# Augmented q and k on all 128 partitions, in a kernel of attention, a mixing MLP and gated expert attention

## The chip, the cores and the metric

The kernel runs on one core of one Trainium2 chip. The metric is the device time of one execution in microseconds (us); less is better. The five engines of the core run side by side, each through its own instructions in a fixed order, and wait for each other by semaphores: TensorE (PE: matrix products, which go to PSUM), VectorE (DVE), ScalarE (ACT), GpSimd (POOL) and SyncE (SP, which here issues most DMAs).

## The reference, cut to what matters

Three blocks follow each other. The first is causal attention with a forget gate, over 4 batches of 8 heads with 576 positions and head width 64:

```python
scores = scale * np.matmul(q, k.transpose(0, 1, 3, 2))
cum = np.cumsum(np.log(np.clip(f, 0.0001, 1.0)), axis=-1)
decay = cum[:, :, :, None] - cum[:, :, None, :]
scores = np.where(causal, -1000000000.0, scores + decay)
scores = scores - np.max(scores, axis=-1, keepdims=True)
attn = np.exp(scores)
attn = attn / (np.sum(attn, axis=-1, keepdims=True) + 1e-09)
return np.matmul(attn, v).astype(np.float32)
```

The second takes x (4 x 576 x 512), mixes positions by U and V (rank 32) and applies an MLP of width 2048: `u + np.maximum(u @ w_ch1, 0.0) @ w_ch2`. The third has four experts, each a causal attention with head width 64 and no decay, of which a gate picks two per position: `out += mask[..., None] * w[:, :, kk:kk + 1] * ye`.

## The kernel before, in words

Every float32 value that is multiplied is split into a high part that TensorE's format holds and a low rest, so most products come in threes (high by high, high by low, low by high).

A head has four tiles (make_heads, L115): qa and ka hold the high parts of q and k in partitions 0 to 63, qb and kb hold the low and high parts for the two cross products, on all 128 partitions. qa and ka are augmented: partitions 64 and 65 of ka hold the negated cumulative log gates (high and low), against ones in qa, which adds the column part of the decay inside the score product; partition 66 of qa holds the row's maximum, against -1 in ka, which subtracts it. AUG is 67: score products of qa and ka contract 67 partitions, those of qb and kb 128. The partitions behind AUG aren't read. In the expert block partitions 64 and 65 of ka are zero.

For each head row_max (L151) first forms all scores of the causal triangle on 66 partitions (ua, ub) and VectorE takes their maxima with a mask (L159, L177) into a column tile mx; TensorE transposes it (mt, L182), VectorE makes the row mr of it (L184), and two DMAs put mr into partition 66 of qa (L186, L187). Then scores (L190) forms the transposed scores again in two PSUM tiles: for u = 0 five products, for u = 1 twelve (L213), of qa by ka, qb by kb and the mask. ScalarE takes the exponential (pf, L222) and its half-precision part (ph, L223), VectorE the rest (pl, L224). weighted_values (L230) multiplies by the values (av, 45 products per head), and normalise (L287) writes x. Per head, 1600 columns of scores and 1600 columns of row maxima are products of qa and ka, 1600 of qb and kb, 576 of the mask, and some 2900 of av.

log_sums (L476) is the first thing in the program: it loads f, clips it (L484), takes the logarithm on ScalarE (L485), scans it on VectorE (L486), splits the result into chl (L487, L488), stores it (L490) and feeds partitions 64 and 65 of the first ka tiles by DMA (L549). Meanwhile load_pair (L518) loads q, k (qkt) and v (vr) of two heads by one pair of DMAs, split_high (L528) casts them on ScalarE, split_low (L540) copies rows by DMA and forms the low parts on GpSimd, and value_scale (L248) finds a power of two for v: a reduce (L251), a transpose by TensorE (amt), three small steps and a reciprocal, and the scaling of vr (L270).

first_batch (L701) works through the 8 heads of the first batch; mix (L582) turns each pair's x into u (gp, up), and behind it the weights of the MLP are loaded, and narrowed from the 64-bit words of their layout by steps on VectorE and ScalarE (L308 to L311; wst). later_batches (L735) puts the products of the MLP (hps, L399: hidden; cps, L414: output, evacuated by L416) between the heads of the other three batches. Behind the heads, at some 400 us, the rest of the MLP runs alone; then the expert block, from some 695 us, with six heads' tiles (heads2, two heads, made at some 400 us; heads3, four heads, made when the MLP's pools are released).

TensorE's order is written out by hand (manual_schedule). The order on VectorE, ScalarE, GpSimd and SyncE's queue is set by the framework's scheduler, which runs its own timeline model over the program; so an added instruction can change the order of others.

Of the kernel before, what the change touches and what calls it, by code (L numbers as in the profile page):

```python
# [18 lines left out]
P = 128  # L19
B, H, S, D = 4, 8, 576, 64  # L20
# [7 lines left out]
HC = 288  # L28
# [1 line left out]
KT = DM // P  # L30
NQ = 4
FT = FF // P // NQ
AUG = 67
NH2A = 2
NH2B = 4
PSCALE_LN = 8.0 * math.log(2.0)
# [14 lines left out]
M_LO = [0, 64, 192, 320, 448]  # L51
# [3 lines left out]
def f32(ap):  # L55
    return ap.bitcast(F32)
# [3 lines left out]
def kernel(  # L60
# [13 lines left out]
    nc = tc.nc  # L74
# [4 lines left out]
    def pool(name, bufs=1, side="left", space=None):  # L79
        kw = {} if space is None else {"space": space}  # L80
        if space is None:
            kw["side"] = side
            kw["reuse_waits"] = "tile"
        return tc.alloc_tile_pool(name=name, bufs=bufs, **kw)
# [27 lines left out]
    ones1 = const.tile([1, P], BF16, name="ones1")  # L112
    nc.gpsimd.memset(ones1[:], 1.0)

    def make_heads(pl_, n, decay):  # L115


        made = []
        for i in range(n):
            qa = pl_.tile([P, S], F32R, name=f"qa{i}")  # L120
            qb = pl_.tile([P, S], F32R, name=f"qb{i}")
            ka = pl_.tile([P, SP_], F32R, name=f"ka{i}")
            kb = pl_.tile([P, SP_], F32R, name=f"kb{i}")
            nc.gpsimd.memset(f32(qa[64:AUG, :]), 1.0)
            nc.gpsimd.memset(f32(ka[:, S:SP_]), 0.0)
            nc.gpsimd.memset(f32(kb[:, S:SP_]), 0.0)
            nc.gpsimd.memset(f32(ka[64:AUG, :S]), -1.0)
            if not decay:
                nc.gpsimd.memset(f32(ka[64:66, :S]), 0.0)
            made.append((qa, qb, ka, kb))  # L130
        return made

# [18 lines left out]
    def row_max(hb, mx, apart=False):  # L151


        qa, qb, ka, kb = hb
        ua = ps2.tile([P, 2, 512], F32, name="ua", tag="s2")
        for c0, c1 in ((0, HC), (HC, S)):
            nc.tensor.matmul(ua[:, c0 // HC, 0:HC], qa[0:66, M_LO[4]:S], ka[0:66, c0:c1],
                             start=True, stop=True)
        nc.vector.tensor_tensor_reduce(  # L159
            ua[:, :, 0:HC], ua[:, :, 0:HC],  # L160
            maskm[:].rearrange("p (c n) -> p c n", c=2), 1.0, NEG, OP.add, OP.max, mx[:, 4:5])
        if apart:
            yield
        ub = ps2.tile([P, 2, 512], F32, name="ub", tag="s2")
        where = {3: (0, 0), 0: (0, 448), 2: (1, 0), 1: (1, 320)}
        for t in (3, 2, 1, 0):
            bk, off = where[t]
            w = M_W[t]
            n = 64 if t == 0 else P
            nc.tensor.matmul(ub[0:n, bk, off:off + w], qa[0:66, M_LO[t]:M_LO[t] + n],  # L170
                             ka[0:66, 0:w], start=True, stop=True)
        for t in (3, 2, 1, 0):
            bk, off = where[t]
            w = M_W[t]
            n = 64 if t == 0 else P
            m0 = S - P if t == 0 else S - w
            nc.vector.tensor_tensor_reduce(  # L177
                ub[0:n, bk, off:off + w], ub[0:n, bk, off:off + w], maskm[0:n, m0:m0 + w], 1.0, NEG,
                OP.add, OP.max, mx[0:n, t:t + 1])
        yield  # L180
        mt = psf.tile([NT, P], F32, name="mt", tag="f")
        nc.tensor.transpose(mt[:], mx[:], ident[:])  # L182
        mr = small.tile([NT, P], F32R, name="mr", bufs=2)
        nc.vector.tensor_scalar(mr[:], mt[:], PSCALE_LN / ISC, None, OP.subtract)  # L184
        row = f32(qa[66:67, :])
        nc.sync.dma_start(row[:, 0:64], f32(mr[0:1, 0:64]))  # L186
        cur["last"] = nc.sync.dma_start(row[:, 64:S].rearrange("o (t p) -> o t p", p=P),  # L187
                                        f32(mr[1:NT, :]))

    def scores(hb):  # L190

        qa, qb, ka, kb = hb
        ph = cur["att"].tile([P, 1600], F16, name="ph")
        pl = cur["att"].tile([P, 1600], F16, name="pl")
        for u in range(2):
# [6 lines left out]

            todo = []
            for some in (pieces[:-1], pieces[-1:]):
                todo += [(ka[0:AUG, jt * P:jt * P + P], qa[0:AUG, i0:i0 + w], bk, off, w)
                         for jt, i0, bk, w, off in some]
                todo += [(kb[:, jt * P:jt * P + P], qb[:, i0:i0 + w], bk, off, w)
                         for jt, i0, bk, w, off in some]
# [3 lines left out]
            for n, (wa, xa, bk, off, w) in enumerate(todo):  # L212
                nc.tensor.matmul(ps[:, bk, off:off + w], wa, xa, start=bk not in banks[:n],  # L213
                                 stop=bk not in banks[n + 1:])
            if u == 0:
                todo = ((ps[:, :, 0:HC], 0, S),)
            else:
                todo = ((ps[:, 0, :], S, 512), (ps[:, 1, :], S + 512, 512))
# [278 lines left out]
    sin = pool("sin", 1)  # L497
    att = pool("att", 2)
    hpool = pool("heads1")
    heads = make_heads(hpool, 4, True)  # L500
    att0 = pool("att0", 1, "right")
    pf0 = pool("pf0", 3, "right")
    cur["pf"] = pf0
# [313 lines left out]
    hpool = pool("heads2")  # L817
# [24 lines left out]
                            fill=0.0, base=0, channel_multiplier=0)  # L842
    every = sw.tile([P, P], BF16, name="every")
    nc.gpsimd.memset(every[:], 1.0)
    heads = make_heads(hpool, NH2A, False)
    def load_y(b, yp, stp, tag):
        yh = yp.tile([P, KT, SP_], F32R, name="yh", tag="yh")
        yl = yp.tile([P, KT, SP_], F32R, name="yl")
# [15 lines left out]
    hpool2 = pool("heads3", 1, "right")  # L864
    att = pool("att2", 2, "right")
    cur["att"] = cur["pf"] = att
    sy = pool("sy", 2, "right")
    ys = [sy0, pool("sy1", 1, "right")]
    heads += make_heads(hpool2, NH2B, False)

    def gates(lg, cf):

# [339 lines left out]
```

## Time and profile before

| What | us |
|---|---|
| timed runs: lowest, median, highest of 3 | 910.83, 911.1, 919.22 |
| profiled execution, its own time | 907.14 |
| its span, first to last instruction | 905.4 |
| TensorE busy in the span | 836.5 |
| VectorE busy | 543.4 |
| ScalarE busy | 429.0 |
| GpSimd busy | 304.8 |

The profile is of one execution; its own time is the span and what lies around it. All times of instructions are counted from the start of the span. Busy time is the time in which an engine has an instruction under way; products of TensorE overlap, so the time of one product as listed is longer than what it adds. The granted clock is the share of full speed that TensorE was given: 1.00 is 2.4 GHz, 0.50 is 1.2 GHz.

### The profile page before, as it was taken

What the parts mean: (1) busy time and instruction counts of PE and PEld (TensorE: products, weight loads), DVE (VectorE), ACT (ScalarE), POOL (GpSimd) and SP (SyncE); (2) the same over time, 40 slices, a digit from 0 to 9 for tenths busy, and PEclk for the clock granted to TensorE, in tenths of its full rate; (3) what the DMA queues carried; (4) which work ended last, traced back from release to release, by engine and by line L of the source; (5) the groups of instructions that cost most, each with busy time, mean ns of one, the idle gap of its engine ahead of it and who ended that gap; (6) DMA issues with size and microseconds to landing.
All of it is one profiled execution on the core that took longest, in us unless ns stands there. A gap on an engine that the chain in (4) does not pass through costs nothing.

```text
span 905.4 us, 19022 instructions
## 1 busy us (share of the span) xinstructions
PE 836.5 (92%) x7476; PEld 785.1 (87%) x7476; DVE 543.4 (60%) x1464; ACT 429.0 (47%) x836; POOL 304.8 (34%) x283
## 2 busy tenths in 40 slices
PE   2888599989999999989999999999999999999997
PEld 2777498879999989989989999999999888989775
DVE  6789879986667756632254722222223768787654
ACT  3667566655544554332255622322112576665553
POOL 9556654443322442012145422523103241311000
PEclk9987779999999999999999999999999999999999
DMA  6335565453432442003169742433103231321222
GB/s 190 113 98 139 160 214 172 150 176 92 115 100 84 133 121 63 27 18 115 53 228 340 237 163 91 129 109 126 54 27 92 54 86 41 88 45 30 73 89 71
DMA packets 68809, 101.94 MB, mean 113 GB/s; under 512 B 6640, under 2 KB 49456, under 8 KB 68720
## 3 DMA queue, kind: packets, MB, share of 16 engines
q1 hardware_dynamic: 64448, 92.47, 34.1%
q10 hardware_dynamic: 4272, 8.26, 2.5%
q8 instruction: 59, 0.97, 0.4%
q14 instruction: 30, 0.25, 0.1%
HBM read 60.33 MB, written 22.56 MB: 92 GB/s over the span
## 4 chain that ended last, share of the span: by engine, by line
PE 69%; DVE 13%; DMA 8%; ACT 5%; issue 3%; SPq 1%; POOL 1%; ACTq 0%; DVEq 0%; POOLq 0%
PE cps L414 20%; PE hps L399 18%; PE sc L213 9%; PE pq L917 4%; PE po L1029 3%; DMA raw<-in_w_dram 3%; DVE pl L224 3%; PE av L240 2%; PE pv L982 2%; PE gp L588 2%; PE ub L170 2%; DVE ub L177 2%; ACT pf L222 2%; PE av L244 2%; PE av L242 2%
## 5 line engine op out<-in xcount | busy, mean ns | idle before, releaser
L414 PE MATMUL cps<-hh,w2h 128*128 128x288 f32 x512 | 155.7, 304 | 3.6 <-DVE hl L404 3.4
L224 DVE TENSOR_TENSOR pl<-pf,ph 128x576 f16<-128x576 f32 x144 | 124.8, 869 | 47.3 <-ACT ph L223 47.2
L414 PE MATMUL cps<-hh,w2l 128*128 128x288 f32 x512 | 152.3, 297 | 0.0
L414 PE MATMUL cps<-hl,w2h 128*128 128x288 f32 x512 | 151.6, 296 | 0.0
L399 PE MATMUL hps<-uh,w1h 128*128 128x288 f32 x512 | 144.2, 303 | 0.0
L404 DVE SCALAR_TENSOR_TENSOR hl<-hps,hh 128x288 fp32r<-128x288 f32 x128 | 58.2, 455 | 142.0 <-ACT hh L403 142.0
L399 PE MATMUL hps<-uh,w1l 128*128 128x288 f32 x512 | 141.1, 298 | 0.0
L403 ACT ACTIVATE hh<-hps 128x288 fp32r<-128x288 f32 x128 | 52.4, 409 | 182.9 <-PE hps L399 182.9
L222 ACT ACTIVATE pf<-sc 128x576 f32<-128x576 f32 x144 | 83.8, 612 | 41.6 <-PE sc L213 34.9
L414 PEld LDWEIGHTS cps<-hh,w2h 128*128 128x128 f32 x512 | 97.3, 190 | 4.7 <-DVE hl L404 4.5
L399 PEld LDWEIGHTS hps<-uh,w1h 128*128 128x128 f32 x512 | 97.3, 190 | 0.2 <-DVE hl L404 0.2
L399 PEld LDWEIGHTS hps<-uh,w1l 128*128 128x128 f32 x512 | 97.4, 190 | 0.0
L414 PEld LDWEIGHTS cps<-hh,w2l 128*128 128x128 f32 x512 | 97.1, 190 | 0.0
L414 PEld LDWEIGHTS cps<-hl,w2h 128*128 128x128 f32 x512 | 97.0, 189 | 0.0
L213 PE MATMUL sc<-qa,ka 67*128 67x288 f32 (+4 forms) x288 | 77.8, 330 | 15.0 <-DMA qa<-mr 7.7
L223 ACT CAST ph<-pf 128x576 f16<-128x576 f32 x144 | 89.1, 638 | 1.5
L240 PE MATMUL av<-vh,ph 128*128 128x65 f16 x720 | 88.1, 204 | 1.5 <-DVE x L287 1.5
L399 PE MATMUL hps<-ul,w1h 128*128 128x288 f32 x512 | 87.9, 294 | 0.0
L242 PE MATMUL av<-vl,ph 128*128 128x64 f16 x720 | 86.8, 199 | 0.0
L244 PE MATMUL av<-vh,pl 128*128 128x65 f16 x720 | 86.6, 199 | 0.0
L177 DVE CUSTOM_DVE_ANT_0 ub<-ub,maskm 128x448 f32<-128x448 f32 x192 | 81.4, 424 | 8.2 <-PE ub L170 7.0
L385 POOL TENSOR_TENSOR ul<-ust,uh 128x1152 fp32r<-128x1152 f32 x18 | 48.2, 2676 | 89.4 <-ACT uh L384 84.8
(182 smaller groups left out, 1986.7 us busy)
## 6 DMA issues: line engine op xcount, KB each, us to landing
raw<-in_w_dram SPq DMA_DIRECT2D x32, 512.0 KB
ust<-udram SPq DMA_DIRECT2D x20, 576.0 KB
qkt<-in_qk_dram SPq DMA_DIRECT2D x16, 576.0 KB
yc<-ydram SPq DMA_DIRECT2D x14, 576.0 KB
ydram<-yc SPq DMA_DIRECT2D x14, 576.0 KB
vr<-in_v_dram SPq DMA_DIRECT2D x16, 320.0 KB
udram<-ustage ACTq DMA_DIRECT2D x16, 288.0 KB
ydram<-ust SPq DMA_DIRECT2D x8, 576.0 KB
```

The lines of the kernel that those rows point to most:

```text
L177: nc.vector.tensor_tensor_reduce(ub[0:n, bk, off:off + w], ub[0:n, bk, off:off + w], maskm[0:n, m0:m0 + w], 1.0, NEG, OP.add, OP.max, mx[0 ...
L213: nc.tensor.matmul(ps[:, bk, off:off + w], wa, xa, start=bk not in banks[:n], stop=bk not in banks[n + 1:])
L222: nc.scalar.activation(pfv, view, AF.Exp, scale=ISC)
L223: nc.scalar.copy(ph[:, o0:o0 + n], pf[:, 0:n])
L224: nc.vector.tensor_tensor(pl[:, o0:o0 + n], pf[:, 0:n], ph[:, o0:o0 + n], OP.subtract)
L240: nc.tensor.matmul(av[0:m, it, :], ph[0:k, c:c + m], vh[0:k, jt, :], start=first, stop=False)
L242: nc.tensor.matmul(av[0:m, it, 0:64], ph[0:k, c:c + m], vl[0:k, jt, :], start=False, stop=False)
L244: nc.tensor.matmul(av[0:m, it, :], pl[0:k, c:c + m], vh[0:k, jt, :], start=False, stop=last)
L399: nc.tensor.matmul(ph[:], wa[:, k, fs], xa[:, k, :], start=n == 0, stop=n == 3 * KT - 1)
L403: nc.scalar.activation(hh[:], ph[:], AF.Relu)
L404: nc.vector.scalar_tensor_tensor(hl[:], ph[:], 0.0, f32(hh[:]), OP.max, OP.subtract)
L414: nc.tensor.matmul(pc[:], wa[:, t, dsl], xa[:], start=n == 0, stop=n == 3 * FT - 1)
```

## The change

qa and ka are filled on all 128 partitions, and AUG becomes 127: the row's maximum goes to partition 127 of qa (against -1 in ka), the decay stays in partitions 64 and 65. Partitions 66 to 95 have ones in qa and zeros in ka, partitions 96 to 126 zeros in qa and -1 in ka, so all of them add zero. The row-max products contract 127 partitions in place of 66, the score products of qa and ka 128 in place of 67. Each head's two tiles get two memsets on GpSimd (32 x 576 each, in place of 3 x 576; the separate zeroing of partitions 64 and 65 in the expert block is gone) and two on VectorE (32 x 576 each).

```diff
-AUG = 67
+AUG = 127
...
-    def make_heads(pl_, n, decay):
+    def make_heads(pl_, n):
...
-            nc.gpsimd.memset(f32(qa[64:AUG, :]), 1.0)
+            nc.gpsimd.memset(f32(qa[64:96, :]), 1.0)
+            nc.vector.memset(f32(qa[96:P, :]), 0.0)
             nc.gpsimd.memset(f32(ka[:, S:SP_]), 0.0)
             nc.gpsimd.memset(f32(kb[:, S:SP_]), 0.0)
-            nc.gpsimd.memset(f32(ka[64:AUG, :S]), -1.0)
-            if not decay:
-                nc.gpsimd.memset(f32(ka[64:66, :S]), 0.0)
+            nc.gpsimd.memset(f32(ka[64:96, :S]), 0.0)
+            nc.vector.memset(f32(ka[96:P, :S]), -1.0)
             made.append((qa, qb, ka, kb))
         return made
...
-            nc.tensor.matmul(ua[:, c0 // HC, 0:HC], qa[0:66, M_LO[4]:S], ka[0:66, c0:c1],
+            nc.tensor.matmul(ua[:, c0 // HC, 0:HC], qa[0:AUG, M_LO[4]:S], ka[0:AUG, c0:c1],
                              start=True, stop=True)
...
-            nc.tensor.matmul(ub[0:n, bk, off:off + w], qa[0:66, M_LO[t]:M_LO[t] + n],
-                             ka[0:66, 0:w], start=True, stop=True)
+            nc.tensor.matmul(ub[0:n, bk, off:off + w], qa[0:AUG, M_LO[t]:M_LO[t] + n],
+                             ka[0:AUG, 0:w], start=True, stop=True)
...
-        row = f32(qa[66:67, :])
+        row = f32(qa[AUG:P, :])
...
-                todo += [(ka[0:AUG, jt * P:jt * P + P], qa[0:AUG, i0:i0 + w], bk, off, w)
+                todo += [(ka[:, jt * P:jt * P + P], qa[:, i0:i0 + w], bk, off, w)
                          for jt, i0, bk, w, off in some]
...
-    heads = make_heads(hpool, 4, True)
+    heads = make_heads(hpool, 4)
...
-    heads = make_heads(hpool, NH2A, False)
+    heads = make_heads(hpool, NH2A)
...
-    heads += make_heads(hpool2, NH2B, False)
+    heads += make_heads(hpool2, NH2B)
```

The order of TensorE's instructions stays as it is. On the other engines the scheduler makes another order at several places. VectorE at the start of the program, before (pa, pb and chl belong to log_sums; am, ar, rs and vr to the scale of v):

```order
L483 MEMSET pa 32x576
L99 CAST identb<-ident 128x128
L484 TENSOR_SCALAR pa<-pa 32x576
L486 SCALAR_TENSOR_TENSOR pb<-pa 32x576
L487 TENSOR_SCALAR chl<-pb 32x576
L488 SCALAR_TENSOR_TENSOR chl<-pb,chl 32x576
L251 TENSOR_REDUCE am<-vr 128x1
L256 TENSOR_REDUCE ar<-amt 1x1
L257 TENSOR_SCALAR ar<-ar 1x1
L258 TENSOR_SCALAR ar<-ar 1x1
L251 TENSOR_REDUCE am<-vr 128x1
L265 RECIPROCAL rs<-rsp 128x1
```

And now, from the last of eight such memsets that stand behind that of pa:

```order
L129 MEMSET ka_167 32x576
L99 CAST identb<-ident 128x128
L484 TENSOR_SCALAR pa<-pa 32x576
L251 TENSOR_REDUCE am<-vr 128x1 x2
L256 TENSOR_REDUCE ar<-amt 1x1
L257 TENSOR_SCALAR ar<-ar 1x1
L258 TENSOR_SCALAR ar<-ar 1x1
L265 RECIPROCAL rs<-rsp 128x1
L270 TENSOR_SCALAR vr<-vr,rs 128x640
L486 SCALAR_TENSOR_TENSOR pb<-pa 32x576
L487 TENSOR_SCALAR chl<-pb 32x576
L488 SCALAR_TENSOR_TENSOR chl<-pb,chl 32x576
```

The eight memsets stand ahead of the clip of pa, and the scan and chl have moved behind both reduces and the scaling of the first v. ScalarE at the start, before (L485 is the logarithm; the casts are those of the first and then of the second pair of heads):

```order
L485 ACT_TABLE_LOAD
L485 ACTIVATE pa<-pa 32x576
L535 CAST qa_135<-qkt 64x576
L536 CAST ka_137<-qkt 64x576
L537 CAST qb_144<-qkt 64x576
L538 CAST kb_146<-qkt 64x576
L535 CAST qa_151<-qkt 64x576
L536 CAST ka_153<-qkt 64x576
L537 CAST qb_160<-qkt 64x576
L538 CAST kb_162<-qkt 64x576
```

And now:

```order
L535 ACT_TABLE_LOAD
L535 CAST qa_135<-qkt 64x576
L536 CAST ka_137<-qkt 64x576
L537 CAST qb_146<-qkt 64x576
L538 CAST kb_148<-qkt 64x576
L535 CAST qa_155<-qkt 64x576
L536 CAST ka_157<-qkt 64x576
L537 CAST qb_166<-qkt 64x576
L538 CAST kb_168<-qkt 64x576
L485 ACT_TABLE_LOAD
L485 ACTIVATE pa<-pa 32x576
```

The logarithm has moved behind all eight casts, and a table load is added. VectorE at some 400 us, where the last head of the last pair is normalised (den, rn, x) and the last mix (g) begins, before:

```order
L278 TENSOR_SCALAR den<-av,rs 128x5
L281 RECIPROCAL rn<-den 128x5
L287 TENSOR_TENSOR x<-av,rn 128x5x64
L404 SCALAR_TENSOR_TENSOR hl<-hps,hh 128x288
L592 TENSOR_TENSOR g<-gp,g 32x128
```

And now:

```order
L278 TENSOR_SCALAR den<-av,rs 128x5
L125 MEMSET qa_8026 32x576
L129 MEMSET ka_8028 32x576
L125 MEMSET qa_8036 32x576
L129 MEMSET ka_8038 32x576
L281 RECIPROCAL rn<-den 128x5
L404 SCALAR_TENSOR_TENSOR hl<-hps,hh 128x288
L287 TENSOR_TENSOR x<-av,rn 128x5x64
L592 TENSOR_TENSOR g<-gp,g 32x128
```

The four memsets of heads2 stand between den and rn, and hl goes ahead of x.

## Rows read from the trace of the kernel before

**Rows 1.** The page: TensorE's busy time, and its granted clock in 40 slices.

```profile
PE 836.5 (92%) x7476; PEld 785.1 (87%) x7476; DVE 543.4 (60%) x1464; ACT 429.0 (47%) x836; POOL 304.8 (34%) x283
...
PEclk9987779999999999999999999999999999999999
```

**Rows 2.** Busy time by stretch: length, engines with instructions, clock, DMA share, GB/s.

```profile
20.00:46.00 26.00, 21.36 (x139) 18.88 (x140) 17.93 (x53) 16.70 (x30) 15.23 (x14) 1.00 0.45 134
...
50.00:56.00 6.00, 5.85 (x46) 5.24 (x45) 3.09 (x10) 4.01 (x7) 1.40 (x1) 0.50 0.02 6
...
109.60:124.80 15.20, 15.19 (x97) 13.60 (x98) 10.31 (x27) 8.33 (x17) 9.67 (x7) 0.50 0.48 148
...
200.00:380.00 180.00, 176.81 (x1791) 164.44 (x1790) 119.91 (x352) 89.45 (x171) 57.09 (x37) 1.00 0.33 100
```

**Rows 3.** Chain of waits: start, length, piece; shares by line, 13-62 and 108-127.

```profile
23.85 2.74 PE sc L213 x12
...
60.16 1.57 PE sc L213 x12
...
109.62 2.68 PE gp L588 x10
...
241.14 1.50 PE gp L588 x10
...
by line: PE sc L213 33.6%; DMA qa<-mr 14.5%; ACT pf L222 6.7%; PE ub L170 6.4%; issue 5.4%; DMA ur<-in_u_dram 4.7%; PE av L240 4.6%; DVE ub L177 4.2%; PE av L244 3.2%; PE av L242 3.1%; DVE ua L159 2.9%; PE gp L588 2.7%; PE mt L182 1.6%; SPq
...
by line: PE sc L213 27.7%; PE hps L399 14.2%; PE gp L588 14.1%; PE av L240 6.2%; PE up L600 6.0%; issue 5.9%; PE ub L170 4.5%; PE av L244 4.3%; PE av L242 4.3%; PE ua L157 4.1%; ACT pf L222 3.1%; DVE x L287 2.5%; PE up L597 2.5%; PE mt L182
```

**Rows 4.** TensorE in order of time: start, length, line, rows*columns, shape.

```profile
30.74 0.44 PE L213 MATMUL sc<-qb,kb 128*128 128x288 f32 x1
30.98 0.44 PE L213 MATMUL sc<-qa,ka 67*128 67x288 f32 x1
```

**Rows 5.** The same view of ScalarE, VectorE, SyncE's queue and TensorE, first 13 us.

```profile
0.80 1.28 ACT L485 ACT_TABLE_LOAD   x1 [0.80 <-PEq L1198]
3.54 0.68 ACT L485 ACTIVATE pa<-pa 32x576 f32<-32x576 f32 x1 [1.45 <-DVE pa L484]
...
11.03 0.66 ACT L538 CAST kb<-qkt 64x576 fp32r<-64x576 f32 x1
...
0.98 0.54 DVE L483 MEMSET pa<- 32x576 f32 x1 [0.98 <-PEq L1198]
...
4.25 1.35 DVE L486 TENSOR_TENSOR_SCAN pb<-pa 32x576 f32<-32x576 f32 x1 [0.75 <-ACT pa L485]
...
6.31 0.75 DVE L488 SCALAR_TENSOR_TENSOR chl<-pb,chl 32x576 fp32r<-32x576 f32 x1
...
10.27 0.82 DVE L251 TENSOR_REDUCE am<-vr 128x1 f32<-128x640 f32 x1 [1.29 <-DMA vr<-in_v_dram]
...
11.20 1.55 DVE L270 TENSOR_SCALAR vr<-vr,rs 128x640 f32<-128x640 f32 x1
12.67 0.75 DVE L159 CUSTOM_DVE_ANT_0 ua<-ua,maskm 128x576 f32<-128x576 f32 x1
...
8.00 1.42 SPq L549 DMA_DIRECT2D ka<-chl  x2
...
10.78 0.82 PE L157 MATMUL ua<-ka,qa 66*128 66x288 f32 x2 [1.59 <-DMA ka<-chl]
```

**Rows 6.** The same view at 401 us: VectorE's last x and TensorE's last gp.

```profile
401.63 0.49 DVE L287 TENSOR_TENSOR x<-av,rn 128x320 f32<-128x320 f32 x1
...
402.61 1.42 PE L588 MATMUL gp<-x,ut 128*96 128x128 f32 x10
```

**Rows 7.** The same view at 689 us: one of VectorE's last evacuations of cps.

```profile
689.48 0.46 DVE L416 TENSOR_TENSOR yc<-cps,yc 128x288 f32<-128x288 f32 x1 [1.14 <-PE cps L414]
```

**Rows 8.** The same view of TensorE from 96 to 111 us, where it waits.

```profile
99.67 1.22 PE L170 MATMUL ub<-ka,qa 66*128 66x448 f32 x4 [2.60 <-ACT pf L222]
...
109.61 1.81 PE L588 MATMUL gp<-x,ut 128*96 128x128 f32 x7 [4.79 <-DVE ar L257]
```

## The prediction

> **What bounds the kernel now.** I read the page first: TensorE is busy 836.5 us of the 905.4 us span, and the line of its granted clock is below nine tenths only in the third to sixth of the 40 slices of 22.6 us, which lie at 45 to 136 us [rows 1]. So the change can act on the clock only in the first batch and a little behind it. Then I read the busy time by stretches: from 200 to 380 us the engine is busy 176.81 of 180 us at 1.00, and there is nothing for a clock to give back; from 50 to 56 us and from 109.6 to 124.8 us it is busy nearly all the time and has 0.50, the lower of the two levels, 1.2 GHz [rows 2]. The same view says 1.00 from 20 to 46 us, which must not be believed: twelve score products take 2.74 us at 23.85 on the chain of waits and 1.57 us at 60.16 [rows 2, 3]. Work of the same kind in the 0.50 stretch has the longer time too (the ten products of gp take 2.68 us at 109.62 and 1.50 us at 241.14) [rows 3]. So the engine stands at 1.2 GHz from its first products on; the column only knows of changes that were recorded. The chain also says what is bound by it: TensorE's lines have 55% of the 49 us from 13 to 62, and 90% of the 19 us from 108 to 127 [rows 3].
>
> **The padding itself.** 66 or 67 rows become 127 or 128. A product of 288 columns takes 0.44 us with 67 rows and 0.44 us with 128, side by side [rows 4], so no product gets longer or shorter: 0 us. No product is added, and TensorE's order is the same.
>
> **The start, +8.0 us.** The eight new memsets of the first four heads stand on VectorE behind the memset of pa, ahead of the rest of log_sums. One of this shape takes 0.54 us [rows 5], eight take 4.3 us, from 1.5 to 5.9 us. That alone is hidden. What isn't is what the scheduler then does: VectorE reduces both v tiles and scales the first before it comes to the scan (L486), and ScalarE makes the eight casts of both q/k pairs, then loads a table, and only then takes the logarithm (L485). Before, the logarithm started at 3.54 and took 0.68, and the scan began at 4.25. Now:
> ScalarE: the last cast ends at 11.03 + 0.66 = 11.69, the added table load takes 1.28, the logarithm 0.68: 13.65.
> VectorE: the second v lands at 10.27; its reduce ends at 11.09; the small steps and the reciprocal take some 0.9 (an estimate, from the gap to 11.20 and their sizes), the scaling 1.55: 13.6.
> The two ends agree by chance, so moving one of them back would not help. From 13.65 the scan and what hangs on it run as before: chl was done at 6.31 + 0.75 = 7.06, or 2.81 after the scan began, so it is now done at 16.46. SyncE issued the decay rows 0.94 us after chl (L549, 8.00), and the row-max products started 2.78 us after that issue, at 10.78, and took 0.82. All that together: the products are there at 21.0 in place of 11.6. VectorE, though, began the first maximum only at 12.67, since it was scaling v; so the loss is 21.0 - 12.67 = 8.3 us, of which I take 8.0, since SyncE is freer then [all rows 5]. Behind this maximum stand the maximum's row, its two DMAs and the first score product, and each next head waits for the one ahead. The bounds are 5 (inputs of the third pair are now issued ahead of the first maximum's DMAs and may give some back) and 9.4 (the whole shift of chl).
>
> **Between the big stages, +2.2 us.** The four memsets of heads2 stand between den and rn of the last pair's last head. Before, x was written from 401.63, and the gp products started at 402.61 after a group of hidden products that covers the wait [rows 6]. Four times 0.54 less some overlap is 2.0 us, of which that cover hides 0.1: +1.9, bounds 0 and 2.2. The eight of heads3 stand ahead of the last four evacuations of cps, each of which waits 1.14 us for TensorE before it runs 0.46 [rows 7]. They take 4.3 us in place of the 1.14 us of idle time before the first; three PSUM buffers and the idle time of the next ones take up nearly all of it: +0.3, bounds 0 and 2.
>
> **The first batch's order, -3 us.** TensorE waits for ScalarE's pf until 99.67, and 4.79 us until 109.61 for VectorE [rows 8]. In the new order one set of weight narrowing (L308 to L311) fewer stands on VectorE ahead of the x for that second wait, and on ScalarE the pf goes ahead of a step of it, rather than behind. Some 2 us for the first wait and 1 us for the second; as this hangs on when weights land, the bounds are -5 and +2.
>
> **The clock, -8 us.** The chain has 27 us of TensorE from 13 to 62, less some 4 at 2.4 GHz behind 57, and 17 from 108 to 127, less 1.6 behind 124.8: 38.5 us at 1.2 GHz. By 1.57 / 2.74 the higher level would save 43% of that, 16.5 us [rows 3]; that is the end if the clock is up from the first product on. The other end is 0, or a few us of loss if it falls oftener. What speaks for a gain is that the engine was without a gap from 109.6 to 124.8 and stayed at 1.2 GHz, in work with much of 66 and 67 rows; from 200 to 380 us the same heads are mixed with hidden and output products of 128 rows, and there it never falls [rows 2]. Of a head's 8276 columns 3200 are narrow ones (1600 each of qa against ka in scores and row max), the rest is filled already, so the padding can only tip stretches that are near. I take half: -8.
> The Trainium skill, page "TensorE: Matmul & The Clock Gate", section "What's actually happening", says that the gate is set by how busy TensorE has been of late, and says nothing of rows. By that the padding would leave the clock where it is, and the sum would be without this term. The 15.2 us without a gap at 0.50 do not fit busy time alone [rows 2], but no run here has changed the rows only.
>
> **The sum.** +8.0 + 1.9 + 0.3 - 3.0 - 8.0 = -0.8 us on the profiled execution's 907.1 us. This execution is 4 us below the median of the timed runs, 911.1; put on the median it makes 910.3.
>
> **The rivals.**
> Slower, the clock doesn't follow rows. Then the late start decides alone: +7.2 us, 918.3 us, and 914 to 923 with the bounds of the order. Its place is the first maximum at 12.67; it wins once the clock gives back less than 7.2 us. For it speaks that the added waits are certain, as the queues are in order, while the gain is inferred; and that over 60% of a head's columns have 128 rows already and the clock was low with them. Against it the stretch from 109.6. By the skill's rule this is the outcome.
> Faster, the clock comes up with the first scores and stays: -16.5 in place of -8, -9.3 in all, 901.8 us. Against it: from 13 to 62 TensorE is on the chain only 55% of the time, it waits for DMAs and exponentials (21.36 us busy of 26 from 20 to 46 [rows 2]), and at the higher level the same work would leave it waiting for more of the time.
> The start is hidden: if the loads that now come earlier give back 3 of the 8 us, the forecast becomes 907 us. This is a lower edge of the forecast rather than a case of its own.
>
> **How the numbers follow.** The forecast has 0.5, the slower rival 0.37, the faster 0.13. About 1% (9.1 us) is what a measurement of this kernel can tell from no change; that puts the borders at 902.0 and 920.2. Over the upper one lie a third of the slower rival and a fifth of the forecast's own spread (the ends of the start, order and clock terms): 0.12 + 0.10, rounded up to 0.24, as every unlisted stall is on this side. Under the lower one lie two thirds of the faster rival and an eighth of the forecast: 0.15. Within 1% remain 0.61. The range reaches to most of both: 900 to 921; the forecast's own is 904 to 916.
>
> **What would show it.** The first score product should start at about 28 us in place of 20 and the first maximum at about 21; if they start where they did, the start term is wrong. Gp of the last pair should start near 404.5 less the shift of all. In the first batch twelve score products should take 1.57 us more often than 2.74, above all in what was 109.6 to 124.8; if they take 2.74 as often as now, the clock term is wrong and the slower rival holds. The stretch from 200 to 380 us should look as it does. The forecast as a whole is wrong if the span changes by over 1% either way.

## The result, and the profile after

The changed kernel takes 922.45 us in the median of 17 runs (917.58 to 924.08), the kernel before in the same comparison 911.58 (905.70 to 919.22): a ratio of 1.0103, 95% interval 1.0080 to 1.0127. It is slower by about 1%, some 9 to 11 us; the forecast was 910.3. The profiled execution took 922.25 us with a span of 920.5, so it stands at the median of its kernel, while that of before (907.14) is one of the shorter of its own. A difference of the two profiles is therefore some 4 us too large, and where a size matters below, the ratios of timed runs decide.

The page of the changed kernel, busy time and granted clock:

```profile
PE 830.2 (90%) x7476; PEld 777.9 (85%) x7476; DVE 560.0 (61%) x1484; ACT 430.5 (47%) x837; POOL 300.4 (33%) x277
...
PEclk9989789999999999988999999999999999999999
```

TensorE is busy 6.3 us less than before and the span is 15.1 us longer [rows 1]. That is not a slower TensorE but a waiting one. The line of the clock has a new pair of eights in the 18th and 19th slice, which lie at 391 to 437 us, where before it had nines.

Busy time by stretch, columns as in rows 2:

```profile
109.60:124.80 15.20, 8.76 (x49) 7.30 (x50) 13.93 (x26) 8.59 (x16) 9.34 (x7) 0.66 0.45 128
200.00:380.00 180.00, 175.54 (x1761) 163.12 (x1759) 121.88 (x344) 90.61 (x174) 59.32 (x39) 1.00 0.35 102
405.00:420.00 15.00, 12.94 (x79) 11.66 (x76) 4.16 (x10) 1.47 (x4) 0.00 (x0) 0.66 0.11 33
...
60.00:80.00 20.00, 16.87 (x218) 14.90 (x218) 18.82 (x59) 14.94 (x28) 10.59 (x8) 1.00 0.31 81
47.00:210.00 163.00, 134.56 (x1399) 119.74 (x1398) 147.03 (x374) 108.04 (x204) 90.21 (x62) 0.92 0.54 161
```

From 200 to 380 us all is as before [rows 2]. From 109.6 to 124.8 the engine is busy 8.76 us at 0.66, where it was busy throughout at 0.50; other work stands there now, and part of it still runs at the lower level. From 405 to 420 us, where before the engine had 1.00, it has 0.66.

The start, the same view as in rows 5, of ScalarE, VectorE, GpSimd, SyncE's queue and TensorE:

```profile
11.34 1.28 ACT L485 ACT_TABLE_LOAD   x1
12.63 0.68 ACT L485 ACTIVATE pa<-pa 32x576 f32<-32x576 f32 x1
...
13.94 2.54 DVE L486 TENSOR_TENSOR_SCAN pb<-pa 32x576 f32<-32x576 f32 x1
16.51 1.47 DVE L487 TENSOR_SCALAR chl<-pb 32x576 fp32r<-32x576 f32 x1
18.02 1.83 DVE L488 SCALAR_TENSOR_TENSOR chl<-pb,chl 32x576 fp32r<-32x576 f32 x1
23.25 0.77 DVE L159 CUSTOM_DVE_ANT_0 ua<-ua,maskm 128x576 f32<-128x576 f32 x1 [3.40 <-PE ua L157]
...
15.34 2.33 POOL L556 TENSOR_TENSOR kb<-qkt,ka 64x576 fp32r<-64x576 f32 x1
...
22.65 0.37 SPq L523 DMA_DIRECT2D qkt<-in_qk_dram  x1
28.15 0.58 SPq L186 DMA_DIRECT2D qa<-mr  x1
...
22.27 0.82 PE L157 MATMUL ua<-ka,qa 127*128 127x288 f32 x2 [10.24 <-DMA ka<-chl]
```

The logarithm comes behind the eight casts and the table load, as worked out, and the scan starts at 13.94 (forecast 13.65). But the scan and the two steps of chl took 5.91 us together, where before they took 2.81 [rows 5], and so chl is ready at 19.85, not at 16.46. In the new place they run beside GpSimd's 64x576 steps; before, they ran beside GpSimd's short memsets. Before, for the same steps:

```profile
5.63 0.65 DVE L487 TENSOR_SCALAR chl<-pb 32x576 fp32r<-32x576 f32 x1
...
15.55 1.41 POOL L556 TENSOR_TENSOR kb<-qkt,ka 64x576 fp32r<-64x576 f32 x1
```

The Trainium skill, page "SBUF — State Buffer", section "SBUF: two separate sides", says that VectorE and GpSimd share a pair of ports to SBUF which, for some kinds of instruction, one of them holds for a whole instruction. The longer times of both engines here agree with it (L487 1.47 us in place of 0.65, L556 2.33 in place of 1.41).

The first maximum starts at 23.25, 10.6 us later than before, and the first score product at 30.66 (forecast about 28). In two further profiles with this order of the start the scan took 1.60 and 1.85 us and the first transposition came 9.2 and 9.1 us late, so the loss at the first head is 9.1 to 10.6 us. The sign that the prediction gave for the clock shows only faintly in this profile: of the first ten heads' groups of twelve score products six take over 2.5 us before and four now, and the one at 118 us, in the stretch named first, is still one of them.

The place near 401 us, the same view as in rows 6:

```profile
406.19 0.22 DVE L278 TENSOR_SCALAR den<-av,rs 128x5 f32<-128x5 f32 x1 [2.01 <-PE av L244]
406.59 0.54 DVE L125 MEMSET qa<- 32x576 f32 x1 [0.17 <-issue]
...
408.98 0.19 DVE L281 RECIPROCAL rn<-den 128x5 f32<-128x5 f32 x1
409.67 0.46 DVE L404 SCALAR_TENSOR_TENSOR hl<-hps,hh 128x288 fp32r<-128x288 f32 x1 [0.50 <-ACT hh L403]
410.04 0.48 DVE L287 TENSOR_TENSOR x<-av,rn 128x320 f32<-128x320 f32 x1
...
406.83 0.44 PE L399 MATMUL hps<-uh,w1l 128*128 128x288 f32 x1
...
410.58 1.50 PE L588 MATMUL gp<-x,ut 128*96 128x128 f32 x10 [1.39 <-DVE x L287]
...
403.70:405.60 1.90, 1.36 (x38) 1.27 (x39) 0.48 (x1) 0.00 (x0) 0.52 (x2) 1.00 0.10 39
405.75:409.05 3.30, 3.30 (x21) 3.09 (x17) 2.45 (x6) 0.00 (x0) 0.00 (x0) 0.50 0.00 0
409.20:412.45 3.25, 1.50 (x10) 1.14 (x10) 0.90 (x3) 0.67 (x2) 0.00 (x0) 1.00 0.00 0
412.60:419.25 6.65, 6.50 (x26) 6.03 (x27) 0.55 (x2) 0.80 (x2) 0.00 (x0) 0.50 0.16 48
```

The four memsets stand between den and rn, hl waits 0.50 us for ScalarE ahead of x, x starts at 410.04, and TensorE waits 1.39 us for it. The clock is at the lower level twice (the last four lines are busy time by stretch, columns as in rows 2). The first fall, at 405.7, comes ahead of the first of these memsets, so they did not make it. The second comes behind the wait: from 409.2 to 412.45 TensorE is busy 1.50 of 3.25 us at 1.00, and from 412.6 to 419.25 it has 0.50. A product of 288 columns takes 0.44 us in both, the time at 1.2 GHz [rows 4]; before, the same products took 0.29.

To read where time goes, the start of each head's transposition (mt, L182) is set against before; a table of the differences in us, worked out from the timelines (heads 0 to 31 are the first stage, 32 to 47 the experts; the rows below the first are of the experiments that follow):

```
head                        0     10     17     31     32     37     47
after                    10.6    5.9    5.1    4.9   12.5   12.5   16.5
67 rows, order of after  10.6   11.6   13.0   13.1   21.9   22.1   25.2
128 rows, order before    0.0    0.9    0.5   -0.4    1.3    0.8    3.8
same with the memsets     4.5    4.5    3.9    3.6   10.1   10.0   10.0
zero rows by GpSimd      -0.2   -1.0   -2.0   -2.4   -2.0   -3.0   -1.6
```

After: +10.6 at the start, 5.7 given back in the first batch, +7.5 between heads 31 and 32, +4 in the expert block. The 7.5 are two places: by the starts of the same products of TensorE, 6.1 us arise at some 400 us, where heads2 is made, and 1.5 at some 690 us, where heads3 is made. At the second place eight memsets stand ahead of the evacuations of cps (yc, L416), and TensorE waits for one of these, which it did not do before:

```profile
703.73 0.54 DVE L129 MEMSET ka<- 32x576 f32 x1
704.30 1.19 DVE L416 TENSOR_TENSOR yc<-cps,yc 128x288 f32<-128x288 f32 x3
...
704.81 0.40 PE L414 MATMUL cps<-hh,w2h 128*128 128x288 f32 x1 [1.21 <-DVE yc L416]
```

### The profile page after: what moved, and what is told of

The parts are those of the page before. It is cut to its first block, busy times and chain, and to the rows that moved or that the text cites. A ratio compares the mean times of both kernels' runs of the same rounds, so it can differ in the third digit from the quotient of the medians.

```text
span 920.5 us, 19041 instructions
## 1 busy us (share of the span) xinstructions
PE 830.2 (90%) x7476; PEld 777.9 (85%) x7476; DVE 560.0 (61%) x1484; ACT 430.5 (47%) x837; POOL 300.4 (33%) x277
## 4 chain that ended last, share of the span: by engine, by line
PE 63%; DVE 18%; DMA 9%; ACT 5%; issue 3%; SPq 1%; POOL 0%; ACTq 0%; DVEq 0%; POOLq 0%
PE cps L414 18%; PE hps L399 18%; PE sc L213 7%; PE pq L917 4%; DVE pl L224 4%; PE po L1029 3%; DMA raw<-in_w_dram 3%; DVE ub L177 2%; PE av L240 2%; PE gp L588 2%; PE pv L982 2%; DMA ust<-udram 2%; PE ub L170 2%; PE av L244 1%; DMA yst<-ydram 1%
## 5 line engine op out<-in xcount | busy, mean ns | idle before, releaser
L213 PE MATMUL sc<-qa,ka 128*128 128x288 f32 (+4 forms) x288 | 75.8, 324 | 19.2 <-DMA qa<-mr 12.0
L240 PE MATMUL av<-vh,ph 128*128 128x65 f16 x720 | 83.4, 199 | 1.5 <-DVE x L287 1.5
L242 PE MATMUL av<-vl,ph 128*128 128x64 f16 x720 | 82.1, 195 | 0.0
L244 PE MATMUL av<-vh,pl 128*128 128x65 f16 x720 | 81.9, 195 | 0.0
```

The lines of the kernel that those rows point to most:

```text
L240: nc.tensor.matmul(av[0:m, it, :], ph[0:k, c:c + m], vh[0:k, jt, :], start=first, stop=False)
L242: nc.tensor.matmul(av[0:m, it, 0:64], ph[0:k, c:c + m], vl[0:k, jt, :], start=False, stop=False)
L244: nc.tensor.matmul(av[0:m, it, :], pl[0:k, c:c + m], vh[0:k, jt, :], start=False, stop=last)
```

## The experiments

Theory A: the loss is the memsets on VectorE and the order they bring; the rows do nothing. Theory B: the rows act on the clock, also in the last stage, where they cost. Theory C, formed after the first four runs: the rows give time in the first batch through the clock, and the memsets and the order cost more than that. Each ratio is to the kernel before on the same chip, with its 95% interval; runs on different chips are compared through the kernel before, which ran beside each. The clock is the median of the mean granted clocks of the timed runs.

**One part alone.** The padding without VectorE's memsets (the rows add one constant to a row's scores and its maximum, which the softmax drops):

```diff
-AUG = 67
+AUG = 127
-            nc.gpsimd.memset(f32(qa[64:AUG, :]), 1.0)
+            nc.gpsimd.memset(f32(qa[64:P, :]), 1.0)
-            nc.gpsimd.memset(f32(ka[64:AUG, :S]), -1.0)
+            nc.gpsimd.memset(f32(ka[64:P, :S]), -1.0)
```

> The products on all 128 rows (the row of maxima in row 127, the added rows multiplying 1 by -1, which adds one constant to every score and to its maximum), with the GpSimd memsets of the kernel before made taller and no memset on VectorE. Theory A (the loss is the memsets on VectorE and the order that they bring; the rows cost and gain nothing): first maximum at 12.7 within 0.5 us, no step between the last head of the hidden batch and the first of the next stage (under 1 us), no steps at the third head of each later batch; 0.997 to 1.004 of before. Theory B (the rows act on the clock): the three steps of 1.2 to 1.5 us in the last stage stand, the first batch is 5 us shorter, with the start as before; 0.995 to 1.000 with the clock low at about 406 and at three places behind 760.

906.38 us, 0.9944 (0.9908 to 0.9980), clock 0.975 against 0.968: faster than theory A allows, and a little faster than theory B's range. In its profile, the second longest of its ten executions, the start is that of before, but the first batch is not shorter, and a step of 1.45 us at head 38 stands although there are no memsets on VectorE.

The memsets without the padding: after, with the products on `qa[0:66]` and `ka[0:67]` as before.

> The 20 memsets of the change on VectorE and the taller ones on GpSimd, but all products on 66 and 67 rows as before. Theory A: the first maximum starts at 23 within 1 us, the step of 7 us at the second heads is there, the time is that of after within 3 us (920 to 925 us, 1.008 to 1.014). Theory B: the start is as late as in after, but without rows the later steps (7.5 us between the two stages, three times 1.3 us) are gone or halved: 912 to 917 us.

939.37 us, 1.0286 (1.0246 to 1.0327), clock 0.956: outside both ranges. The scheduler had made a third order of the first batch for it, so two things had changed at once.

After, with the first heads' eight memsets on GpSimd, and with the second heads' four:

```diff
-            nc.vector.memset(f32(qa[96:P, :]), 0.0)
+            zero.memset(f32(qa[96:P, :]), 0.0)
-            nc.vector.memset(f32(ka[96:P, :S]), -1.0)
+            zero.memset(f32(ka[96:P, :S]), -1.0)
-    heads = make_heads(hpool, NH2A)
+    heads = make_heads(hpool, NH2A, nc.gpsimd)
```

> After, with the eight new memsets of the first four heads on GpSimd; those of the second and third set stay on VectorE. Theory A: first maximum back at 12.7 to 14, the shift of 5 us behind the first batch falls to 0 to 1 us, the rest of after's loss stays (7 at the second heads, 4 in the last stage): about 917 to 919 us. Theory B (first batch gains by the rows): behind the first batch the heads stand 3 to 6 us earlier than before, 911 to 914 us.

920.27 us, 1.0102 (1.0063 to 1.0141). The first transposition is back at 16.1 us, yet behind the first batch the heads stand 9.2 us late, so both theories missed. The scheduler had made a new order of the batch here too, and that this ate the gain was not tested by itself. The run tells nothing of the start's price.

> After, with the four new memsets of the second set of heads on GpSimd, nothing else. Theory A: den and rn follow one another again, the clock stays up at 406, the step between the stages falls from 7.5 to at most 1 us, 915 to 917 us. A rival of it (the clock falls there for another reason, the rows or what went before): the step stays at 5 us or more and the clock is low at 406 to 419 as in after; 920 to 922 us.

917.30 us, 1.0054 (1.0025 to 1.0084). The step between heads 31 and 32 is 1.2 us in place of 7.5, and the clock is 1.00 where after had 0.66. At 400 us nothing is left of after's 6.1 us. But the scheduler has also put hl behind x again, so the 0.5%, some 4.5 us, are the price of the four memsets and of hl ahead of x together; all else on the engines has the order of after. The eight memsets of the third heads are still on VectorE, and the 1.5 us at 690 us stand as in after.

**Rows and order taken apart.** From here on, but for the last run, the order is held: every instruction of an engine gets an edge to the one ahead of it in a given list, which orders the queue and waits for nothing.

```diff
+    def pin(order):
+        for row in order:
+            for a, b in zip(row[:-1], row[1:]):
+                tc.add_manual_dep(traced[b], a, ...)
```

> After, with every instruction on VectorE, ScalarE, GpSimd and SyncE held in the order that after has them, all memsets included, but the products on 66 and 67 rows as before. Theory A (rows are worth nothing, the 28 us of the run with memsets only came from its other order in the first batch): 920 to 925 us, heads 3 to 17 shifted as in after within 2 us. Theory C (the rows give time in the first batch, through the clock): 928 to 940 us, the same shift of 10.6 us at the first head, no give-back of 5.6 us behind it, and the clock low for longer between 60 and 210.

> Before, with every instruction held in the order of before, but the products on all 128 rows (as in the padding-only run). Theory A: 909 to 913 us, every head within 2 us of before. Theory C: 895 to 906 us; the gain of 5 us or more stands between the 3rd and the 17th head, with twelve score products at 1.5 to 1.6 us where before has 2.7.

```
                      67 rows                            128 rows
order of before    1       clock 0.964     0.9937 (0.9914 to 0.9960)  clock 0.973
order of after     1.0160  clock 0.963     1.0103 (1.0080 to 1.0127)  clock 0.975
                  (1.0120 to 1.0199)
```

927.63 and 906.79 us. In either order the rows bring 0.6%, 5 to 6 us, with a clock higher by 0.009 to 0.012; in either kind of rows the memsets and the order of after cost 1.6 to 1.7%, some 15 us. Within the noise the two do not disturb each other. This is theory C, with a gain a little short of what it expected. That holding an order costs nothing was not tested alone; but in the first line of the table the kernel on 128 rows is the held one and in the second the kernel on 67 rows, so a cost or gain of holding would push the two differences apart, and they agree. Nor does it matter much what the added rows hold: in the order of before they multiply 1 by -1, in the order of after one of the two factors is zero. Where the gain stands is read in the pair in the order of after; the profile of 67 rows:

```profile
60.00:80.00 20.00, 19.33 (x158) 16.95 (x157) 14.00 (x42) 11.49 (x23) 8.10 (x7) 0.60 0.26 68
...
47.00:210.00 163.00, 140.18 (x1309) 124.83 (x1308) 145.00 (x355) 104.67 (x198) 86.86 (x60) 0.81 0.51 149
```

From 60 to 80 us TensorE is busy 19.33 us at 0.60 and gets 158 products done; after, with 128 rows, 16.87 us at 1.00 for 218. From 47 to 210 us the clock is 0.81 against 0.92. By head 31 the pair differs by 8.1 us (13.1 against 4.9 in the table), more than the 5.2 of the ratios; this profiled execution, 932.5 us, was the longest of its six, 4.9 above their median. The profile of 128 rows in the order of before (911.1 us) was likewise the longest of its twelve, and its table row shows no gain; the timed runs do. The Trainium skill, page "TensorE: Matmul & The Clock Gate", section "What's actually happening", says that the gate follows how busy the engine is, and names no rows; here the same instructions in the same order had the higher clock with more rows, and the measurement decides.

**The memsets at their places, all else in the order of before.**

> After (128 rows, 20 memsets on VectorE at the places where after has them), but everything else held in the order of before. If the memsets themselves make the start late: the row of decay waits for 4.3 us of memsets, first maximum at 16 to 17 us in place of 12.7 (before) and 23.3 (after). If only the reordering does: first maximum at 12.7 to 13.5. Either way the step at the second heads of 7 us stands. Time: that of the run on 128 rows in the order of before, plus 4 to 8 at the start as far as it isn't given back, plus 7.

916.65 us, 1.0026 (1.0000 to 1.0051): 0.9% or 8 us behind the same rows without them, a little less than expected. VectorE at its start:

```profile
1.68 0.54 DVE L125 MEMSET qa<- 32x576 f32 x1 [0.16 <-issue]
...
6.64 0.91 DVE L484 TENSOR_SCALAR pa<-pa 32x576 f32<-32x576 f32 x1
8.30 1.35 DVE L486 TENSOR_TENSOR_SCAN pb<-pa 32x576 f32<-32x576 f32 x1 [0.75 <-ACT pa L485]
9.68 1.47 DVE L487 TENSOR_SCALAR chl<-pb 32x576 fp32r<-32x576 f32 x1
11.19 1.85 DVE L488 SCALAR_TENSOR_TENSOR chl<-pb,chl 32x576 fp32r<-32x576 f32 x1
...
16.46 0.77 DVE L159 CUSTOM_DVE_ANT_0 ua<-ua,maskm 128x576 f32<-128x576 f32 x1
```

The clip of f (L484) waits behind the memsets until 6.64, where before it ran at 2.77, and the first maximum comes at 16.46 in place of 12.67. The memsets by themselves are not hidden: they cost 3.8 us there, and between heads 31 and 32 4.9 us more than the same rows without them. The scan, from 8.30 to 9.65, runs all but its end ahead of GpSimd's first 64x576 step, which begins at 9.34, and takes its old 1.35 us; the two steps of chl beside those steps take the long times again.

**The start of before, the order of after behind it.**

> After, with the order of before up to the first maximum (13 us), four of the first eight memsets in idle gaps of VectorE there and four behind the first row of maxima, and the order of after from there on. Theory A: first maximum at 12.7 to 13.5; the 5 us that stand behind the first batch in after go to between -5 and 0; 912 to 917 us (the 7.5 us at the second heads and some of the last stage stay). Rival (the first batch is bound by something else, so that an earlier start is eaten up): behind the first batch heads stand as in after within 2 us, 920 to 924 us.

915.17 us, 1.0019 (0.9992 to 1.0045), inside theory A's range, but not for its reason: the first head is where it was before, the second 5.3 us late, and behind the first batch the heads stand 1.0 to 1.3 us late, where theory A had -5 to 0 and its rival some 5. The next two runs are on this.

> The run with the start of before and the order of after from 13 us on, with the memsets of the second and third heads moved to GpSimd: against the run on 128 rows in the order of before (906.8 us) it differs by the first batch's order alone. If that order is worth the 3 us that it was given: 903 to 905 us. If it is worth nothing: 906 to 908. If it costs (the three-part sum of the runs so far asks for some 3 us of cost from it and the third memsets together): 909 to 911 us.

912.57 us, 1.0000 (0.9973 to 1.0028): 0.6% behind the run in the order of before. Not all of it is the first batch: hl still stands ahead of x at 400 us, and 1.7 us arise there. VectorE, SyncE's queue and TensorE in it:

```profile
17.22 0.27 DVE L184 TENSOR_SCALAR mr<-mt 5x128 fp32r<-5x128 f32 x1
...
21.34 0.36 SPq L525 DMA_DIRECT2D vr<-in_v_dram  x1
21.79 0.56 SPq L186 DMA_DIRECT2D qa<-mr  x1
...
25.21 0.58 PE L213 MATMUL sc<-qa,ka 128*128 128x288 f32 x1 [8.37 <-DMA qa<-mr]
```

The row of maxima was ready at 17.5. Its DMA (L186) was issued at 21.79, because two loads of the third pair stand ahead of it in the queue, and they wait until GpSimd has read the first pair's buffers.

> As the run that priced the first batch's order (start of before, late memsets on GpSimd), with the order of before kept up to the first head's row of maxima (20 us): SyncE issues the two DMAs of that row ahead of the third pair's inputs, and VectorE finishes the second head's maxima ahead of the last four of the first memsets. Theory (the 5.4 us that the second head lost in that run were SyncE standing at loads whose buffers GpSimd still read): the first score product starts at 20 us in place of 25.2, and the time falls by 3 to 6 us to 907 to 910. If it stays at 911 to 914, the order of the rest of the first batch costs what was lost, and the time at SyncE was hidden anyway.

912.17 us, 1.0010 (0.9985 to 1.0034): the expected product came, the expected time did not. The same engines in this run:

```profile
22.24 0.42 SPq L641 DMA_DIRECT2D ur<-in_u_dram  x1
...
26.77 0.34 ACT L309 ACTIVATE ur<-ur 128x160 f32<-128x160 f32 x1 [13.26 <-DVE u L308]
...
19.99 0.58 PE L213 MATMUL sc<-qa,ka 128*128 128x288 f32 x1 [3.14 <-DMA qa<-mr]
29.12 1.22 PE L213 MATMUL sc<-qa,ka 128*128 128x320 f32 x3 [7.12 <-ACT pf L222]
```

The first score product starts at 19.99, and then TensorE waits 7.12 us for the exponential: ScalarE stands at the step on ur ahead of it, and ur is loaded by the DMA that is now the one behind the blocked loads. One wait took the other's place. What either run prices, 0.6 to 0.7%, is these loads, the order of the rest of the batch and hl ahead of x (1.7 and 4.4 us at 400 us) together; they were not taken apart.

Neither wait is in after itself. There, with the late start, the loads of the third pair are issued at 22.65 and 23.11, long ahead of the row's DMA at 28.15; the first score product waits 3.18 us for that DMA and the next group 1.73 us for the exponential, against 3.12 and 1.85 before. So what the two spliced runs lost at these places came with the splice, and they do not price the first batch's order as after has it.

**Two last checks of the place and of the gain.**

> After, order held, with the four memsets of the second heads still on VectorE but behind rn and x in place of ahead of them. Theory (what counts is the place, ahead of an x that TensorE waits for, and the fall of the clock that follows): the time of the run with them on GpSimd, 915 to 919 us, the step between the stages 1 to 2 us. Rival (VectorE or the SBUF is held up wherever they stand): 920 to 923 us.

917.69 us, 1.0050 (1.0023 to 1.0077), as with GpSimd, with the clock at 1.00:

```profile
405.00:420.00 15.00, 12.04 (x121) 11.36 (x122) 6.54 (x16) 1.89 (x6) 0.56 (x2) 1.00 0.23 76
```

The same four memsets on the same engine, behind x (and ahead of hl) rather than ahead of rn, cost 0.8 us at 400 us in the profile and nothing that the timed runs can tell. The step between the stages is 3.3 us, more than expected, 1.5 of it at 690 us.

The two places in all profiles, in us against before, by the starts of the same products of TensorE:

```
                                              at 400      at 690
after; 67 rows, order of after                6.1, 6.1    1.5, 1.5
memsets only; first heads on GpSimd           2.4, 5.2    1.5, 1.5
memsets at their places, order of before      4.9         1.5
start of before                               4.4         1.5
second heads on GpSimd; behind x              0.0, 0.8    1.5, 1.5
both late sets on GpSimd, hl ahead of x       1.7, 4.4    0.0, 0.0
128 rows, order of before                     1.4         0.0
padding only; zero rows by GpSimd             0.0, 0.0    0.0, 0.0
```

At 690 us the eight memsets cost 1.5 us in every profile that has them on VectorE, and none has that loss without them. At 400 us, memsets ahead of rn alone cost 4.9 us (order of before), hl ahead of x alone 1.7 and 4.4. The wait itself, up to the start of gp, is 2.2 to 3.2 us of it wherever the memsets stand ahead of x. What comes on top goes with the clock: where it is 0.50 for a while behind gp, as in after, 1.5 to 2.9 us are added; where it stays up (memsets only), the loss stays at 2.4. Why it stayed up there is not known. The 1.4 us of 128 rows in the order of before go with a fall at 398.9 us, ahead of the place and with no memset near.

```diff
+            nc.gpsimd.memset(f32(qa[64:P, :]), 0.0)
+            if decay:
+                nc.gpsimd.memset(f32(qa[64:66, :]), 1.0)
             nc.gpsimd.memset(f32(ka[:, S:SP_]), 0.0)
             nc.gpsimd.memset(f32(kb[:, S:SP_]), 0.0)
+            nc.gpsimd.memset(f32(ka[64:P, :S]), -1.0)
```

> A version for use: rows that add zeros as in after, but written by GpSimd alone (rows 64 to 127 of q zero, its two decay rows one, rows 64 to 127 of k minus one), nothing on VectorE, no order held. Theory (the rows give 5 to 6 us, the memsets on VectorE and the order behind them cost): 903 to 909 us, first maximum at 12.7 within 0.5. Rival (its own order of the first batch undoes it, as in the run with only the first heads on GpSimd): 911 to 918 us.

906.17 us, 0.9916 (0.9887 to 0.9946), clock 0.976: faster than both kernels, and than before by 0.8%. Its profile at the start, and a memset of 64 partitions on GpSimd, which takes the 0.57 us of one of 3:

```profile
2.62 0.57 POOL L124 MEMSET qa<- 64x576 f32 x1
...
19.83 0.58 PE L213 MATMUL sc<-qa,ka 128*128 128x288 f32 x1 [3.14 <-DMA qa<-mr]
```

## Why the prediction was wrong, step by step

The forecast kernel was 0.8 us faster in sum; by the ratio it is 9.4 us slower. The steps that failed are the price of the place at 400 us, which left out hl and the clock behind the wait, the start, which took its durations from another neighbourhood, and the sizes of the clock term and of the third heads' memsets. All missed to the same side. The slower rival's range, 914 to 923, holds the result (by the order's own bounds it begins at 916, not 914), but by luck: its condition, that the clock doesn't follow rows, is false, and the other terms cost what the clock gave.

- **The padding itself, 0 us:** held; products of 288 columns take 0.29 and 0.44 us with 67 and with 128 rows alike.
- **The clock, -8.** The mechanism held, the term was too large: -0.57 to -0.63%, -5.2 to -5.7 us. Half of -16.5 was a choice for whose size no row spoke. That rows would leave the clock where it is, the argument against the term, did not hold here.
- **The first batch's order, -3, bounds -5 and +2: open, even in sign.** With 67 rows in the order of after the heads go from +10.6 at the start to +13.1 at head 31, which would be a loss of 2.4 us; but that execution was 4.9 us above its median. With 128 rows the profiles in the order of after go from +10.6 to +4.9, from +9.2 to +5.4 and from +9.1 to +7.1, those in the order of before from +4.5 to +3.6 and from 0.0 to -0.4; that would be a gain of 1 to 5 us. By the timed runs the order can't be told from 0 or from -3. The two spliced runs don't settle it, as said above.
- **Between the big stages, +1.9, bounds 0 and 2.2: the worst of the sizes.** It costs 4.5 to 4.8 us by the timed runs (0.0049 and 0.0053 of the time), 6.1 in the profile. The step priced the four memsets as a wait of their length, and as a wait that was near: 2.2 to 2.4 us with the memsets alone or without a fall. It left out hl ahead of x, which costs 1.7 us or more alone, and the lower clock behind the wait, where products took 0.44 in place of 0.29 us.
- **The start, +8.0, bounds 5 and 9.4.** Measured 9.1 to 10.6 at the first head. "That alone is hidden", of the memsets, was wrong: alone they move the first maximum by 3.8 us. And the chain was summed with durations from a place where GpSimd was at other work; the scan and the two steps of chl grew by 3.1 us together. How much of the 10.6 reaches the end is known only together with the order: memsets at their places 0.9%, the reordering around them another 0.8% (1.0103 against 1.0026).
- **The third heads' memsets, +0.3, bounds 0 and 2:** 1.5 us. "Take up nearly all of it" was wrong: TensorE waits 1.21 us for an evacuation behind them.

By ratios: rows -0.63%, memsets at their places +0.89%, reordering +0.77%, which makes the +1.03% measured. In the forecast's own terms, of the 10.2 us between it and the result, the clock makes 2.3 to 2.8, the place at 400 us 2.6 to 2.9, the third heads 1.2 and the start 1.1 to 2.6. What is left, 0.7 to 3.0, is all that remains for the first batch's order, and it is less than the width of the result's own interval (7.3 to 11.6 us slower).

Open: the three steps of 1.2 to 1.5 us at heads 38, 42 and 46 in the profile of after. Each stands with a fall of the granted clock to 0.50 for a few us, at 774, 815 and 873 us; the profile of before has none between 755 and 880 us. Of the experiments' profiles all but one have one or two such falls there, and a step with each: with 128 rows and with 67, with memsets on VectorE and without. Only the last of the spliced runs has none, with the same order in that stage as after and as the run on 67 rows. So neither rows nor memsets nor that order alone set them, and what does was not tried. A difference of two profiles in the expert block is therefore no price of an edit. The reordering's 0.8% is for the same reason not placed by one pair of profiles: between after and the run with the memsets in the order of before, 6.1 us stand at the first head, 1.3 at head 31, and 4 arise in the expert block.

## What to carry to other kernels

Fill the partitions of a product when it costs nothing: here 128 rows in place of 67 took the same time per product and gave 0.6% through the clock. Put the fill on an engine that nobody waits for at that moment, and read from the new order who stands behind each added instruction; 2.4 us of memsets ahead of a value that TensorE waits for cost, with the step that went ahead of it too, twice that, and behind it nothing that timed runs could tell. When a scheduler sets the order, hold it before you compare two versions; otherwise each experiment changes the order too. A spliced order can bring waits that neither parent has, so look for its waits in the parents before you take its time as a price.

## What the runs showed that was not expected

- Filled rows go with a higher granted clock: 0.973 and 0.975 against 0.964 and 0.963, in two orders.
- A VectorE step on 32x576 takes 0.65 us beside GpSimd's memsets and 1.47 beside its steps on 64x576 (L487), the scan 1.35 and up to 2.54.
- A memset of 576 columns on GpSimd takes, most times, 0.57 us on 2, 3, 32 and 64 partitions alike.
- In the spliced runs a load whose buffer is still read holds up SyncE's whole queue: 4.3 us for the row of maxima, and, with that out of the way, 7.12 us of waiting for an exponential.
- The clock falls at places where no edit was made: in the last stage the profiles of one kernel or another have none, one, two or three falls to 0.50, each with a loss of 1.2 us or more.
